# Linformer attention and a maxout layer on one core: the first batch in halves of its queries and heads, loads in that order, and a new order of its layers

## Chip, cores, metric

One core of a Trainium2 chip. The metric is device time in microseconds (us) of the whole program, the median over runs. The profile's "span" is one execution from its first to its last instruction, about 2 us less than the time. Engines: TensorE (PE; PEld is its weight load), VectorE (DVE), ScalarE (ACT), GpSimd (POOL, which here issues loads), SyncE (SP, which issues stores). The array is TensorE's matmul array. It is called cold, or at half clock, where a matmul takes twice its time elsewhere, and warm, or at full clock, otherwise; the granted clock is what the profile records of this, 1.00 being full.

## The reference

```python
# q, k, v: (8 batches, 8 heads, 1024, 64); E, F: (64, 1024); w1, w2: (512, 1024); w_out: (1024, 512)
k_proj = einsum('ks,bhsd->bhkd', E, k);  v_proj = einsum('ks,bhsd->bhkd', F, v)
attn = softmax(q @ k_proj^T / 8)                    # 64 keys per head
x    = (attn @ v_proj) as (8192 tokens, 512)
out  = maximum(x @ w1, x @ w2) @ w_out              # float32
```

Both kernels use max(h1, h2) = relu(h1 - h2) + h2. So there is one *up* layer with wd = w1 - w2, and the *down* layer adds relu(...) @ w_out and x @ m, where m = w2 @ w_out is computed once, in batch 0.

## The kernel before

A batch is a list of *slots*, each a few dense matmuls; between them stand the attention steps of the next batch. The program gives each engine its own instructions in a fixed order, its queue. Only batch 0 has nothing to hide its own attention behind. That opening is what the change concerns.

```python
for h0 in (0, H // 2):                          # batch 0: k, v of four heads, then of the other four
    load(tiles[0], "k", k, 0, h0, h0 + H // 2)
    load(tiles[0], "v", v, 0, h0, h0 + H // 2)
for h0 in range(0, H, 2):
    load(tiles[0], "q", q, 0, h0, h0 + 2)       # then q by head pairs
for f0 in range(0, DF, 256): ...                # then w2 and w1 in four pairs of pieces, then w_out
# steps: step_kv projects k and v of all heads; step_kpt and step_qt transpose; step_sc: scores, exp;
# step_da_half: sums and values, Ln, exp(-x), product into xt for one half of the tokens
step_kv(t); step_kpt(t); step_qt(t, 0); step_sc(t, 0)
for p in range(NP2):                            # four head pairs
    if p + 1 < NP2:
        step_qt(t, p + 1); step_sc(t, p + 1)
    step_da_half(t, p, 0)()
    step_w2t(256 * p)                           # transpose a piece of w2 (copy on ACT)
    step_wd(256 * p)                            # w1 - w2 (DVE)
# ... slots of batch 0: 8 up (half 0), m = w2 @ w_out, down (half 0), 8 up (half 1), down (half 1);
#     the second halves of step_da_half between the first up slots
```

The softmax here doesn't subtract the row's maximum and nothing guards it: scores larger than these inputs give would overflow.

## Time and profile before

| | before |
|---|---|
| time, median of 4 runs | 380.91 us (380.29 to 381.39) |
| profiled span | 378.3 us |
| TensorE busy | 353.2 us, 93% |
| first up layer can complete | 40.55 us |
| first up layers of batch 1 start | 92.62 us |
| projection in batch 1 starts | 99.53 us |

From 40.55 us on TensorE does not wait. This is the view of the waits of TensorE between 40 and 95 us, whole; the columns are engine and tile that waited, for whom, us in total, how often, the longest:

```profile
PE mm_ps L280 <- DVE xt_sb L263: 0.8, 1, 0.8
```

That wait is the one that ends at 40.55 us; after it there is none. The reading of the opening is in the prediction.

### The profile page before, as it was taken

The page shows a single profiled execution, that of the slowest core. Times are in us where ns is not written, and L with a number is a line of the kernel's source. Part 1 is how long each engine was busy: PE and PEld are TensorE (multiplying, and loading weights), DVE is VectorE, ACT ScalarE, POOL GpSimd, SP SyncE. Part 2 cuts the span into 40 slices and gives each one's busy share as a digit, 9 for nine tenths or more (in the row PEclk, how much of TensorE's full clock was granted, in tenths as well). Part 3 has the DMA queues.
Part 4 walks back from the last instruction along what each step waited for, and adds up shares of the span by engine and source line. Part 5 has one row for each costly group of instructions (what it writes and reads, how often), then busy time and mean ns, then how long its engine had stood idle before and what let it go on. Part 6 is the DMA issues. An engine that isn't in the chain of part 4 may idle for free.

```text
span 378.3 us, 4743 instructions
## 1 busy us (share of the span) xinstructions
PE 353.2 (93%) x1968; PEld 149.3 (39%) x1968; DVE 149.8 (40%) x211; ACT 152.0 (40%) x202; POOL 31.8 (8%) x44
## 2 busy tenths in 40 slices
PE   2375999999999999999999999999999999999996
PEld 2142344444434344344433444334433443344442
DVE  1034741453608172444425260716245351625040
ACT  1046634455154603653255505551355325460201
POOL 7362010000200002000200011000000000000000
PEclk9998999999999999999999999999999999999999
DMA  8999999969699267965599259936110332020202
GB/s 156 203 197 205 207 207 213 239 116 197 124 198 232 68 166 110 248 117 147 85 224 184 85 139 182 234 88 169 55 57 28 122 74 105 7 81 30 104 27 93
DMA packets 64469, 52.21 MB, mean 138 GB/s; under 512 B 26432, under 2 KB 56128, under 8 KB 64448
## 3 DMA queue, kind: packets, MB, share of 16 engines
q0 software_dynamic: 30304, 28.31, 47.6%
q1 hardware_dynamic: 34144, 23.60, 20.2%
q8 instruction: 15, 0.25, 0.2%
q14 instruction: 6, 0.05, 0.0%
HBM read 57.15 MB, written 16.78 MB: 195 GB/s over the span
## 4 chain that ended last, share of the span: by engine, by line
PE 90%; DMA 3%; ACT 3%; DVE 2%; issue 1%; POOL 1%; ACTq 0%; POOLq 0%
PE mm_ps L301 45%; PE mm_ps L280 30%; PE mm_ps L147 4%; PE att_ps L225 4%; DMA v_sb<-in_v_dram 3%; PE att_ps L206 3%; PE mm_ps L345 2%; ACT ex_sb L214 1%; PE mm_ps L180 1%; DVE qt_sb L187 1%; ACT rech_sb L260 1%; ACT ldh_sb L259 1%; PE att_ps L251 1%; PE mm_ps L161 0%; DVE wd_sb L323 0%
## 5 line engine op out<-in xcount | busy, mean ns | idle before, releaser
L301 PE MATMUL mm_ps<-wo_sb,gt_sb 128*128 128x512 f16 x512 | 123.8, 380 | 0.0
L280 PE MATMUL mm_ps<-xt_sb,wd_sb 128*128 128x512 f16 x512 | 116.6, 380 | 0.8 <-DVE xt_sb L263 0.8
L286 DVE TENSOR_SCALAR gt_sb<-mm_ps 128x512 f16<-128x512 f32 x128 | 87.1, 689 | 40.5 <-PE mm_ps L280 40.5
L237 DVE TENSOR_TENSOR xt_sb<-att_ps,rec_sb 128x1024 f16<-128x1024 f32 x28 | 34.3, 1224 | 113.7 <-ACT rec_sb L234 113.7
L280 PEld LDWEIGHTS <-wd_sb 128*128 128x128 f16 x512 | 47.9, 98 | 61.8 <-issue 7.7
L301 PEld LDWEIGHTS <-gt_sb 128*128 128x128 f16 x512 | 47.8, 98 | 61.9 <-issue 8.5
L301 PE MATMUL mm_ps<-m_sb,xt_sb 128*128 128x512 f16 x256 | 65.9, 380 | 0.0
L308 ACT COPY o_sb<-mm_ps 128x512 f32<-128x512 f32 x64 | 37.3, 582 | 69.9 <-PE mm_ps L301 60.5
L233 ACT ACTIVATE ld_sb<-att_ps 128x1024 f32<-128x1024 f32 x28 | 28.7, 1024 | 55.3 <-PE att_ps L225 55.3
L214 ACT ACTIVATE ex_sb<-att_ps 128x1024 f16<-128x1024 f32 x32 | 32.9, 1027 | 8.6 <-PE att_ps L206 8.6
L301 PEld LDWEIGHTS <-xt_sb 128*128 128x128 f16 x256 | 23.3, 98 | 31.4 <-issue 5.8
L154 ACT CAST kp_sb<-mm_ps 64x512 f16<-64x512 f32 x8 | 4.6, 580 | 63.1 <-PE mm_ps L147 63.1
L234 ACT ACTIVATE rec_sb<-ld_sb 128x1024 f32<-128x1024 f32 x28 | 29.6, 1056 | 0.9
L147 PE MATMUL mm_ps<-k_sb,eft 128*64 128x512 f16 x64 | 17.2, 413 | 6.8 <-DMA k_sb<-in_k_dram 6.8
L90 POOL DMA_DIRECT2D k_sb<-in_k_dram x9 | 7.8, 865 | 155.2 <-PE mm_ps L147 153.3
L206 PE MATMUL att_ps<-qt_sb,kpt_sb 64*64 64x512 f16 x128 | 13.6, 414 | 6.5 <-DVE qt_sb L187 6.5
L147 PE MATMUL mm_ps<-v_sb,eft 128*64 128x512 f16 x64 | 17.0, 413 | 1.9 <-DMA v_sb<-in_v_dram 1.9
L155 DVE CAST vp_sb<-mm_ps 64x512 f16<-64x512 f32 x8 | 5.6, 694 | 26.1 <-ACT kp_sb L154 26.1
L147 PEld LDWEIGHTS <-eft 128*64 128x64 f16 x128 | 7.3, 116 | 17.9 <-issue 13.6
L90 POOL DMA_DIRECT2D q_sb<-in_q_dram x11 | 9.1, 836 | 30.3 <-PE mm_ps L180 29.9
L225 PE MATMUL att_ps<-ex_sb,ones 64*64 64x512 f16 x112 | 11.5, 400 | 0.0
L206 PEld LDWEIGHTS <-kpt_sb 64*64 64x64 f16 x128 | 3.9, 104 | 19.0 <-issue 13.6
(41 smaller groups left out, 126.7 us busy)
## 6 DMA issues: line engine op xcount, KB each, us to landing
out_dram<-o_sb SPq DMA_DIRECT2D x64, 256.0 KB, 2.0
k_sb<-in_k_dram POOLq DMA_DIRECT2D x7, 1024.0 KB, 11.8
v_sb<-in_v_dram POOLq DMA_DIRECT2D x7, 1024.0 KB, 18.2
q_sb<-in_q_dram POOLq DMA_DIRECT2D x7, 1024.0 KB, 21.6
w_sb<-in_moe_w_dram POOLq DMA_DIRECT2D x8, 256.0 KB, 10.4
k_sb<-in_k_dram POOLq DMA_DIRECT2D x2, 512.0 KB, 8.6
v_sb<-in_v_dram POOLq DMA_DIRECT2D x2, 512.0 KB, 10.5
q_sb<-in_q_dram POOLq DMA_DIRECT2D x4, 256.0 KB, 13.5
```

Of the source, the lines that this page charges most:

```text
L90: nc.gpsimd.dma_start(out=t[n][:, h0:h1, :, :], in_=src[b, h0:h1].rearrange("h (p c) d -> p h c d", c=NC),)
L147: nc.tensor.matmul(out=kv_ps[i * KP : (i + 1) * KP, :], lhsT=eft[:, i, c, :], rhs=t[n][:, :, c, :], start=(c == 0), stop=(c == NC - 1),)
L206: nc.tensor.matmul(out=sc_ps[pos : pos + KP, e, :], lhsT=t["kpt"][o * D : (o + 1) * D, 2 * p + e, :], rhs=t["qt"][o * D : (o + 1) * D, 2 * ...
L214: nc.scalar.activation(out=ex, in_=sc_ps, func=ACTF.Exp, scale=scale)
L225: nc.tensor.matmul(out=dst[e * D : (e + 1) * D, o, :], lhsT=ones16[rows, :] if w is None else w[rows, 2 * p + e, :], rhs=ex[rows, e, :], s ...
L233: nc.scalar.activation(out=ld, in_=dn_ps, func=ACTF.Ln)
L234: nc.scalar.activation(out=rec, in_=ld, func=ACTF.Exp, scale=-1.0)
L237: nc.vector.tensor_tensor(out=t["xt"][:, p, :, :], in0=at_ps, in1=rec, op=ALU.mult)
L280: nc.tensor.matmul(out=h_ps, lhsT=wd_sb[:, r, fb * 128 : (fb + 1) * 128], rhs=xt[:, r, j, :], start=(r == 0), stop=(r == NDC - 1),)
L286: nc.vector.tensor_scalar_max(gt[:, fb, :], h_ps, 0.0)
L301: nc.tensor.matmul(out=op_ps, lhsT=lhsT, rhs=rhs, start=(n == 0), stop=(n == NFB + NDC - 1),)
L308: nc.scalar.copy(out=o_sb, in_=op_ps)
```

## The change

Its intent: start the first batch's attention when half of its heads have landed, compute it only for half of the query blocks before the up layers start, and put the rest between up layers. Both up layers then come first, m next, the down layers last. The next batch's attention moves later (slot 23 on, it was 7 on), since its time in the up layers is taken by the second half of this batch.

```diff
+    load(k, heads 0-3); load(v, heads 0-3)
+    load(q, heads 0-3, first half of the query blocks)
+    load(k, heads 4-7); load(v, heads 4-7)
+    load(q, heads 4-7, first half of the query blocks)
     for f0 in range(0, DF, 256):
+        if f0 == 512:
+            load(tiles[0], "q", q, 0, 0, H, NC // 2, NC)      # the other half of q
... (the calls of load are shortened; the cut parts give the steps ranges of heads and blocks)
+    for g in range(2):                                        # two groups of four heads
+        p0 = 2 * g
+        step_kv(t, 4 * g, 4 * g + 4)
+        step_kpt(t, p0, p0 + 2)
+        step_qt(t, 4 * g, 4, 0, NI // 2)
+        step_sc(t, p0, 0)
+        step_sc(t, p0 + 1, 0)
+        if g == 1:
+            step_wd(0)
+        fin = step_da_half(t, p0, 0)
+        fin()
+        if g == 1:
+            step_wd(256)
+        fin = step_da_half(t, p0 + 1, 0)
+        fin()
+    first = {                                                 # what follows which slot
+        0: [(step_wd, 512)],
+        1: [(step_qt, t, 0, 4, NI // 2, NI), (step_sc, t, 0, 1)],
+        2: [(step_qt, t, 4, 4, NI // 2, NI), (step_sc, t, 1, 1), (step_wd, 768)],
+        3: [(step_da_half, t, 0, 1)],  4: [(step_sc, t, 2, 1)],  5: [(step_da_half, t, 1, 1)],
+        6: [(step_sc, t, 3, 1)],  7: [(step_da_half, t, 2, 1)],  9: [(step_da_half, t, 3, 1)],
+    }
... step_w2t copies on DVE instead of ACT; in batch 0:
+            ups = [*up_slots(t, 0), *up_slots(t, 1)]
+            seq = ups[:NFB] + [four step_w2t]
+            seq += ups[NFB:] + [four step_m]
+            seq += [*down_slots(b, t, 0), *down_slots(b, t, 1)]
```

More of the change, by code (lines that the diff above doesn't have):

```diff
@@ L87, in alloc_kvq, with load @@
         return t
-    def load(t, n, src, b, h0, h1):
+    def load(t, n, src, b, h0, h1, c0=0, c1=NC):
         nc.gpsimd.dma_start(
-            out=t[n][:, h0:h1, :, :],
-            in_=src[b, h0:h1].rearrange("h (p c) d -> p h c d", c=NC),
+            out=t[n][:, h0:h1, c0:c1, :],
+            in_=src[b, h0:h1].rearrange("h (p c) d -> p h c d", c=NC)[:, :, c0:c1, :],
         )
     tiles = {0: alloc_kvq()}
-    for h0 in (0, H // 2):
-        load(tiles[0], "k", k, 0, h0, h0 + H // 2)
-        load(tiles[0], "v", v, 0, h0, h0 + H // 2)
-        if h0 == 0:
-            ident = const.tile([128, 128], FP32)
-            make_identity(nc, ident)
-    for h0 in range(0, H, 2):
-        load(tiles[0], "q", q, 0, h0, h0 + 2)
+    load(tiles[0], "k", k, 0, 0, H // 2)
+    load(tiles[0], "v", v, 0, 0, H // 2)
+    ident = const.tile([128, 128], FP32)
+    make_identity(nc, ident)
+    load(tiles[0], "q", q, 0, 0, H // 2, 0, NC // 2)
+    load(tiles[0], "k", k, 0, H // 2, H)
+    load(tiles[0], "v", v, 0, H // 2, H)
+    load(tiles[0], "q", q, 0, H // 2, H, 0, NC // 2)
     w1_sb = const.tile([128, NDC, DF], FP16)
@@ L140, in new_attn, with step_kv, step_kpt @@
         t["xt"] = xpool.tile([128, NP2, 2, HALF], FP16, tag="xt", name="xt_sb")
+        t["qt"] = qtp.tile([128, H, HALF], FP16, tag="qt", name="qt_sb")
         t["ex"] = {}
-    def step_kv(t):
+    def step_kv(t, h0=0, h1=H):
         kv_ps = mm_bank()
+        n = (h1 - h0) * D
         for c in range(NC):
-            for i, n in enumerate(("k", "v")):
+            for i, w in enumerate(("k", "v")):
                 nc.tensor.matmul(
-                    out=kv_ps[i * KP : (i + 1) * KP, :],
+                    out=kv_ps[i * KP : (i + 1) * KP, 0:n],
                     lhsT=eft[:, i, c, :],
-                    rhs=t[n][:, :, c, :],
+                    rhs=t[w][:, h0:h1, c, :],
                     start=(c == 0), stop=(c == NC - 1),
                 )
-        fl = lambda ap: ap.rearrange("p h d -> p (h d)")
-        nc.scalar.copy(out=fl(t["kp"]), in_=kv_ps[0:KP, :])
-        nc.vector.tensor_copy(out=fl(t["vp"][KP:128]), in_=kv_ps[KP:128, :])
-        nc.vector.tensor_copy(out=fl(t["vp"][0:KP]), in_=kv_ps[KP:128, :])
-    def step_kpt(t):
+        fl = lambda ap: ap[:, h0:h1, :].rearrange("p h d -> p (h d)")
+        nc.scalar.copy(out=fl(t["kp"]), in_=kv_ps[0:KP, 0:n])
+        nc.vector.tensor_copy(out=fl(t["vp"][KP:128]), in_=kv_ps[KP:128, 0:n])
+        nc.vector.tensor_copy(out=fl(t["vp"][0:KP]), in_=kv_ps[KP:128, 0:n])
+    def step_kpt(t, p0=0, p1=NP2):
         kpt_ps = mm_bank(FP16)
-        for p in range(NP2):
+        for p in range(p0, p1):
             nc.tensor.transpose(
-                out=kpt_ps[:, p * KP : (p + 1) * KP],
+                out=kpt_ps[:, (p - p0) * KP : (p - p0 + 1) * KP],
                 in_=t["kp"][:, 2 * p : 2 * p + 2, :],
@@ L165, in step_kpt @@
             )
-        src = kpt_ps[:, 0 : NP2 * KP].rearrange("q (p k) -> q p k", k=KP)
-        dst = t["kpt"].rearrange("q (p e) k -> q p e k", e=2)
+        src = kpt_ps[:, 0 : (p1 - p0) * KP].rearrange("q (p k) -> q p k", k=KP)
+        dst = t["kpt"][:, 2 * p0 : 2 * p1, :].rearrange("q (p e) k -> q p e k", e=2)
         for e in range(2):
@@ L174, in step_kpt, with step_qt @@
                 )
-    def step_qt(t, p):
+    def step_qt(t, h0, nh=2, i0=0, i1=NI):
         qt_ps = mm_bank(FP16)
-        for e in range(2):
-            for i in range(NI):
+        ni = i1 - i0
+        for h in range(nh):
+            for i in range(ni):
                 nc.tensor.transpose(
-                    out=qt_ps[:, (e * NI + i) * 128 : (e * NI + i + 1) * 128],
-                    in_=t["q"][:, 2 * p + e, 2 * i : 2 * i + 2, :],
+                    out=qt_ps[:, (h * ni + i) * 128 : (h * ni + i + 1) * 128],
+                    in_=t["q"][:, h0 + h, 2 * (i0 + i) : 2 * (i0 + i) + 2, :],
                     identity=ident16,
                 )
-        if "qt" not in t:
-            t["qt"] = qtp.tile([128, H, HALF], FP16, tag="qt", name="qt_sb")
         nc.vector.tensor_copy(
-            out=t["qt"][:, 2 * p : 2 * p + 2, :].rearrange("q e n -> q (e n)"), in_=qt_ps
+            out=t["qt"][:, h0 : h0 + nh, i0 * 128 : i1 * 128],
+            in_=qt_ps[:, 0 : nh * ni * 128].rearrange("q (h n) -> q h n", h=nh),
         )
     def step_qt_dma(t):
-        t["qt"] = qtp.tile([128, H, HALF], FP16, tag="qt", name="qt_sb")
         nc.sync.dma_start_transpose(
@@ L197, in step_qt_dma, with step_sc @@
         )
-    def step_sc(t, p):
+    def step_sc(t, p, j=None):
         sc_ps = att_banks()
+        n = slice(0, HALF) if j is None else slice(j * HALF // 2, (j + 1) * HALF // 2)
+        w = n.stop - n.start
         for o in range(2):
@@ L206, in step_sc @@
                 nc.tensor.matmul(
-                    out=sc_ps[pos : pos + KP, e, :],
+                    out=sc_ps[pos : pos + KP, e, 0:w],
                     lhsT=t["kpt"][o * D : (o + 1) * D, 2 * p + e, :],
-                    rhs=t["qt"][o * D : (o + 1) * D, 2 * p + e, :],
+                    rhs=t["qt"][o * D : (o + 1) * D, 2 * p + e, n],
                     start=True, stop=True,
@@ L213, in step_sc @@
         t["ex"][p] = ex
-        nc.scalar.activation(out=ex, in_=sc_ps, func=ACTF.Exp, scale=scale)
+        nc.scalar.activation(
+            out=ex[:, :, 0:w], in_=sc_ps[:, :, 0:w], func=ACTF.Exp, scale=scale
+        )
     def step_da(t, p):
@@ L241, in step_da, with step_da_half @@
         return finish
-    def step_da_half(t, p, o):
-        ex = t["ex"][p]
+    def step_da_half(t, p, j):
+        ex = t["ex"].pop(p)
+        W = HALF // 2
         da_ps = att_banks()
         for i in range(2):
-            for e in range(2):
-                r = o ^ e
-                rows = slice(r * KP, (r + 1) * KP)
-                nc.tensor.matmul(
-                    out=da_ps[e * D : (e + 1) * D, i, :],
-                    lhsT=t["vp"][rows, 2 * p + e, :] if i else ones16[rows, :],
-                    rhs=ex[rows, e, :],
-                    start=True, stop=True,
-                )
-        ld = soft.tile([128, HALF], FP32, tag="ldh", name="ldh_sb")
-        rec = soft.tile([128, HALF], FP32, tag="rech", name="rech_sb")
-        nc.scalar.activation(out=ld, in_=da_ps[:, 0, :], func=ACTF.Ln)
+            for r in range(2):
+                for e in range(2):
+                    o = r ^ e
+                    rows = slice(r * KP, (r + 1) * KP)
+                    nc.tensor.matmul(
+                        out=da_ps[e * D : (e + 1) * D, o, i * W : (i + 1) * W],
+                        lhsT=t["vp"][rows, 2 * p + e, :] if i else ones16[rows, :],
+                        rhs=ex[rows, e, 0:W],
+                        start=True, stop=True,
+                    )
+        ld = soft.tile([128, 2, W], FP32, tag="ldh", name="ldh_sb")
+        rec = soft.tile([128, 2, W], FP32, tag="rech", name="rech_sb")
+        nc.scalar.activation(out=ld, in_=da_ps[:, :, 0:W], func=ACTF.Ln)
         nc.scalar.activation(out=rec, in_=ld, func=ACTF.Exp, scale=-1.0)
@@ L263, in finish @@
             nc.vector.tensor_tensor(
-                out=t["xt"][:, p, o, :], in0=da_ps[:, 1, :], in1=rec, op=ALU.mult
-            )
-        return finish
-    def moe_slots(b, t):
-        xt = t["xt"]
-        for j in range(2):
-            gt = gpool.tile([128, NFB, HALF], FP16, tag="gt", name="gt_sb")
-            for fb in range(NFB):
-                def up(fb=fb, j=j, gt=gt):
-                    h_ps = mm_bank()
-                    for r in range(NDC):
-                        nc.tensor.matmul(
-                            out=h_ps,
-                            lhsT=wd_sb[:, r, fb * 128 : (fb + 1) * 128],
-                            rhs=xt[:, r, j, :],
-                            start=(r == 0), stop=(r == NDC - 1),
-                        )
-                    nc.vector.tensor_scalar_max(gt[:, fb, :], h_ps, 0.0)
-                yield up
-            for i in range(NI):
-                cell = {}
-                toks = slice(i * 128, (i + 1) * 128)
-                for part in range(3):
-                    def down(i=i, j=j, gt=gt, cell=cell, toks=toks, part=part):
-                        if part == 0:
-                            cell["ps"] = mm_bank()
-                        op_ps = cell["ps"]
-                        for n in range(4 * part, 4 * part + 4):
-                            if n < NFB:
-                                lhsT, rhs = gt[:, n, toks], wo_sb[:, n, :]
-                            else:
-                                lhsT, rhs = xt[:, n - NFB, j, toks], m_sb[:, n - NFB, :]
-                            nc.tensor.matmul(
-                                out=op_ps, lhsT=lhsT, rhs=rhs,
-                                start=(n == 0), stop=(n == NFB + NDC - 1),
-                            )
-                        if part < 2:
-                            return
-                        o_sb = opool.tile([128, DM], FP32, tag="o", name="o_sb")
-                        nc.scalar.copy(out=o_sb, in_=op_ps)
-                        nc.sync.dma_start(
-                            out=out.rearrange("(n p c) m -> n p c m", p=128, c=NC)[
-                                b, :, 2 * i + j, :
-                            ],
-                            in_=o_sb,
-                        )
-                    yield down
@@ L318 @@
+                out=t["xt"][:, p, :, j * W : (j + 1) * W],
+                in0=da_ps[:, :, W : 2 * W], in1=rec, op=ALU.mult,
+            )
+        return finish
     wd_sb = const.tile([128, NDC, DF], FP16)
@@ L320, with up_slots, up, down_slots @@
     w2t_sb = const.tile([128, NFB, DM], FP16)
+    def up_slots(t, j):
+        W = HALF // 2
+        t["gt", j] = gt = gpool.tile([128, NFB, HALF], FP16, tag="gt", name="gt_sb")
+        for fb in range(NFB):
+            def up(fb=fb):
+                h_ps = mm_bank()
+                for r in range(NDC):
+                    nc.tensor.matmul(
+                        out=h_ps,
+                        lhsT=wd_sb[:, r, fb * 128 : (fb + 1) * 128],
+                        rhs=t["xt"][:, r, :, j * W : (j + 1) * W],
+                        start=(r == 0), stop=(r == NDC - 1),
+                    )
+                nc.vector.tensor_scalar_max(gt[:, fb, :], h_ps, 0.0)
+            yield up
+    def down_slots(b, t, j):
+        for n2 in range(NI):
+            o, i = n2 % 2, 2 * j + n2 // 2
+            cell = {}
+            g0 = (o * 2 + n2 // 2) * 128
+            for part in range(3):
+                def down(o=o, i=i, g0=g0, cell=cell, part=part):
+                    gt = t["gt", j]
+                    if part == 0:
+                        cell["ps"] = mm_bank()
+                    op_ps = cell["ps"]
+                    for n in range(4 * part, 4 * part + 4):
+                        if n < NFB:
+                            lhsT, rhs = gt[:, n, g0 : g0 + 128], wo_sb[:, n, :]
+                        else:
+                            lhsT = t["xt"][:, n - NFB, o, i * 128 : (i + 1) * 128]
+                            rhs = m_sb[:, n - NFB, :]
+                        nc.tensor.matmul(
+                            out=op_ps, lhsT=lhsT, rhs=rhs,
+                            start=(n == 0), stop=(n == NFB + NDC - 1),
+                        )
+                    if part < 2:
+                        return
+                    o_sb = opool.tile([128, DM], FP32, tag="o", name="o_sb")
+                    nc.scalar.copy(out=o_sb, in_=op_ps)
+                    nc.sync.dma_start(
+                        out=out.rearrange("(n p c) m -> n p c m", p=128, c=NC)[
+                            b, :, 2 * i + o, :
+                        ],
+                        in_=o_sb,
+                    )
+                yield down
     def step_wd(f0):
@@ L337, in step_w2t @@
         fb = f0 // 128
-        nc.scalar.copy(
+        nc.vector.tensor_copy(
             out=w2t_sb[:, fb : fb + 2, :].rearrange("q f m -> q (f m)"), in_=ps_t
@@ L353 @@
     new_attn(t)
-    step_kv(t)
-    step_kpt(t)
-    step_qt(t, 0)
-    step_sc(t, 0)
-    for p in range(NP2):
-        if p + 1 < NP2:
-            step_qt(t, p + 1)
-            step_sc(t, p + 1)
-        step_da_half(t, p, 0)()
-        step_w2t(256 * p)
-        step_wd(256 * p)
+    for g in range(2):
[17 more added lines that the diff above has]
+        2: [(step_qt, t, 4, 4, NI // 2, NI), (step_sc, t, 1, 1), (step_wd, 768)],
+        3: [(step_da_half, t, 0, 1)],
+        4: [(step_sc, t, 2, 1)],
+        5: [(step_da_half, t, 1, 1)],
+        6: [(step_sc, t, 3, 1)],
+        7: [(step_da_half, t, 2, 1)],
+        9: [(step_da_half, t, 3, 1)],
+    }
     core = {
@@ L371 @@
     }
-    by_pe = {11: (step_qt, 0), 16: (step_qt, 1), 22: (step_qt, 2), 28: (step_qt, 3)}
+    late = {
+        23: (step_kv,), 24: (step_kpt,), 25: (step_qt, 0), 27: (step_qt, 2), 28: (step_sc, 0),
+        31: (step_da, 0), 32: (step_qt, 4), 33: (step_sc, 1), 36: (step_da, 1),
+        37: (step_qt, 6), 38: (step_sc, 2), 41: (step_da, 2), 43: (step_sc, 3), 45: (step_da, 3),
+    }
     by_dma = {1: (step_qt_dma,)}
@@ L382 @@
             new_attn(nxt)
-            steps = {**core, **(by_dma if b else by_pe)}
-        pending = None
-        for n, slot in enumerate(moe_slots(b, tiles[b])):
-            if b == 0 and n == NFB:
-                for r in range(NDC):
-                    step_m(r)
-            slot()
-            if pending is not None:
-                pending()
-                pending = None
-            if b == 0 and n % 2 == 0 and n < 2 * NP2:
-                pending = step_da_half(tiles[0], n // 2, 1)
-            if n in steps:
-                s = steps[n]
-                pending = s[0](nxt, *s[1:])
+            steps = {n: [(s[0], nxt, *s[1:])] for n, s in (
+                {**core, **by_dma} if b else late).items()}
+        t = tiles[b]
+        if b == 0:
+            ups = [*up_slots(t, 0), *up_slots(t, 1)]
+            seq = ups[:NFB] + [lambda f0=f0: step_w2t(f0) for f0 in range(0, DF, 256)]
+            seq += ups[NFB:] + [lambda r=r: step_m(r) for r in range(NDC)]
+            seq += [*down_slots(b, t, 0), *down_slots(b, t, 1)]
+            steps.update(first)
+        else:
+            seq = [s for j in range(2) for f in (up_slots(t, j), down_slots(b, t, j)) for s in f]
+        pending = []
+        for n, slot in enumerate(seq):
+            slot()
+            for f in pending:
+                f()
+            pending = []
+            for s in steps.get(n, ()):
+                r = s[0](*s[1:])
+                if r is not None:
+                    pending.append(r)
+        for f in pending:
+            f()
         del tiles[b]
```

## The prediction

> **What bounds the kernel now.** I read the page's busy slices first, then the chain of waits in order of time, then the timeline of the first 60 us, then busy time by stretch.
>
> ```profile
> PE   2375999999999999999999999999999999999996
> DMA  8999999969699267965599259936110332020202
> ```
> Each digit is a fortieth of the span (9.46 us), in tenths. TensorE (PE) is full from the fifth slice on; only the first four have room. The stretches agree (start and end, length, then PE busy):
>
> ```profile
> 0.00:13.78 13.78, 2.26 (x16) 1.94 (x17) 1.03 (x3) 1.87 (x2) 8.11 (x16) 1.00 0.99 170
> 13.78:40.55 26.77, 16.84 (x120) 9.06 (x120) 9.09 (x16) 13.37 (x19) 10.56 (x13) 0.94 1.33 202
> 40.55:92.62 52.07, 52.07 (x306) 21.81 (x306) 22.85 (x33) 24.61 (x35) 2.63 (x3) 1.00 1.10 197
> ```
> The third is the rest of batch 0, without a gap in PE. A change of opening can only win in the first 40.55 us. The chain there, with pieces left out:
>
> ```profile
> 4.17 11.98 DMA v_sb<-in_v_dram
> 16.29 3.60 PE mm_ps L147 x15
> 19.91 0.59 ACT kp_sb L154
> ...
> 22.47 0.70 DVE qt_sb L187
> 23.22 0.64 PE att_ps L206 x4
> ...
> 26.30 1.02 ACT ex_sb L214
> 27.32 0.50 ACT ldh_sb L259
> 27.84 0.64 ACT rech_sb L260
> ...
> 39.80 0.70 DVE xt_sb L263
> 40.55 0.38 PE mm_ps L280
> ```
> So: wait to 16.29 for all of k and v (all heads in one projection), then a chain of small steps through ACT, DVE and PE, until the last head pair's xt lets the first up layer finish at 40.55. When loads land shows in whom the issuing engine waited for (bracket: idle before, and what ended it):
>
> ```profile
> 8.58 0.74 POOL L110 DMA_DIRECT2D w_sb<-in_moe_w_dram  x1 [0.84 <-DMA k_sb<-in_k_dram]
> 11.41 0.74 POOL L110 DMA_DIRECT2D w_sb<-in_moe_w_dram  x1 [2.08 <-DMA v_sb<-in_v_dram]
> 17.71 0.74 POOL L110 DMA_DIRECT2D w_sb<-in_moe_w_dram  x1 [0.54 <-DMA q_sb<-in_q_dram]
> 19.05 0.74 POOL L110 DMA_DIRECT2D w_sb<-in_moe_w_dram  x1 [0.60 <-DMA q_sb<-in_q_dram]
> ```
> The first half of k's heads is there at 8.58, of v's at 11.41; each further 512 KB takes about 2.5 us, each 256 KB about 1.3.
>
> **What the Trainium skill says.** "TensorE: Matmul & The Clock Gate", Part 1: the array runs at half clock until a free-running window of about 3.4 us was busy. The trace agrees: k/v pairs of 512 columns start every 0.43 us at 16.3-18.9 and every 0.21 us at 49.5; PE is slow again near 35.3 after idling, and fast from about 38.7. "ScalarE: Activation LUTs", What ACT_TABLE_LOAD costs: an activation with immediate operands takes 186 ns plus 0.833 ns per element, so halving a tile does not halve it. Here 1024 elements took 1.024 us and 512 took 0.595: agreed. "DMA: Bandwidth & Descriptors", Specifications: lines of 512 B or more go at line rate. The quarter loads of q get 512 B lines; the weight pieces have such lines already, and their 256 KB take the same 1.3 us as q's 1 KB lines. So reordering costs no bandwidth. "TensorEngine Tiling (Array Packing)", Key Properties: a change of tiling mode drains the array. Eight down matmuls after such a step take 1.83 us in the chain, 1.73 otherwise; more small steps cost about 0.1 us each.
>
> **The change, part by part.**
>
> *Loads.* k, v of four heads, then a quarter of q, then the same for the other heads, then two weight pairs, the other half of q, two more pairs. Estimated landings from the rates above: k 8.6, v 11.4, q 12.7, k 15.1, v 17.6, q 18.9, weight pairs complete at 21.6 and 24.3, q's rest 26.9, third pair 29.5, fourth 32.2. Bytes are unchanged, so w_out and the next batch land as before.
>
> *Opening.* First group, at the half clock: v at 11.4; 8 pairs of 256 columns, 8 x 0.213 + 0.3 = 2.0, to 13.4; kp cast 0.37 (0.58 less 256 elements) and two transposes, 14.2; meanwhile q's eight transposes (1.04) to 15.2; qt copy 0.69, 15.95; scores, exp from 16.45; two exps of 0.6 to 17.55; sums and values; Ln and exp(-x) of 0.6 + 0.64 per pair, on ACT one after the other to 20.2. PE takes the second projection meanwhile: from 18.2, when the first group's values are out (v landed at 17.6, so the chain and not the DMA sets this), to 20.3. Then the same ladder: kp 20.7, transposes 22.15, qt 22.9, exps 23.4 to 24.5, ACT's Ln/exp for two pairs to 27.15, and on DVE a product (0.6), one wd piece (0.6), the last product, to 27.9. **First up layer complete to go at 28.0 instead of 40.55: 12.5 us earlier.**
>
> *What is given back.* Left for later, in PE time at full clock: w2's transposes 4 x 0.45 = 1.8; half of q's transposes 2 x 0.45 = 0.9; second halves of the scores 4 x 0.23 = 0.9. The later sums and values get cheaper (four 64x64 tiles at once, as in the later batches, where 8 matmuls of 512 take 0.56): 4 x 0.34 instead of 4 x 0.55, -0.8. Net 2.8 us. If PE never waited, the gain would be 12.5 - 2.8 = 9.7.
>
> *Waits that I expect.* DVE runs in order: gt0, wd piece 3 (needs the load of 29.5), gt1, copy of q's second half, and only then the scores of slot 1, which stand ahead of up layer 2 in PE's queue. With gt1 at 30.1-30.75 and the copy to 31.4, PE goes on at 31.45; at full clock it has been through slot 1 and its transposes at 29.65: 1.8 us. Before up layer 8 (second half) DVE still has two products and w2t copies, 0.69 each and moved from ACT: the last product ends about 43.15, PE is there at about 42.1: 1.1 us. At the end of batch 0, the last sums start after slot 45 of 48, and Ln 1.02, exp 1.06, product 1.22 plus 0.5 of latencies (3.8) face two slots of 0.865, the last part of the sums' own matmuls and three up matmuls of 0.216 (together 2.7): about 0.9 us (there were five slots before, no wait). Small-step drains: some eight more at 0.08, 0.6. Sum 4.4: gain **9.7 - 4.4 = 5.3 us** if PE is at full clock when the up layers start. If it is cold (it idles most of 25 to 28), the following 3.4 to 6.8 us run at half speed; part of it lies beside the DVE wait, so it costs up to 1.7 more. Against that, a warm second group would save 0.6, and part of the drains falls in waits. I take 5.3 less 0.6 for the clock plus 0.7 for those: 5.4 us.
>
> *Rest.* Batches 1 to 7 keep their slots, matmul counts and sizes; xt is read as two runs of 256 columns, at the same count of columns. I count zero.
>
> Time: 381.15 - 5.4 = **375.7 us**, 1.4% less.
>
> **The rivals.** (a) *DVE becomes the bound in batch 0's up layers.* Sixteen evictions and four copies, four products, two q copies, two wd pieces: 28 x 0.61 = 17.1 us of DVE, beside 13.8 of up matmuls and about 5.3 of small PE steps, 19.1. So DVE is near the bound but under it; if each order mismatch costs something, gain 2 to 3 us, 378.5. For it: the trace shows 0.61 from start to start for evictions back to back. Against it: seven us of w2 @ w_out and the down layers follow, without DVE work of that size. (b) *The loads set the start anyway.* Weight pairs three and four need bytes that land at 29.5 and 32.2 in any order; if loads slipped 2 us through finer pieces, the up layers stall on DVE and the gain falls to 3.5. For it: DMA is at 9 tenths there. Against it: same bytes and line rates, and the third pair is needed by up layer 4 only. (c) *The opening is gained whole*: warm clock, no wait at the second half, gain 8 to 9, about 372.5. For it: the PE work alone allows 9.7; against it: the three waits above come from the order of instructions, not from luck. (d) *Nothing gained because later waits move up*: the next batch's projections run at slot 23 rather than 7, so loads for batch 3, whose buffers they free, are issued at about 59 instead of 51.7; they are due after 130, so this is hidden.
>
> **Range and chances.** The opening is uncertain by about 1 us each way, the clock by 1.5, the waits by 1.5: gains of 3 to 8 us should hold eight times in ten, 373.2 to 378.1. Faster by over 2% needs more than 7.6 us: 0.16. Slower by over 2% would need a wait in every batch: 0.02.
>
> **What would show it.** Right: the first up matmul with the last xt product near 28 (27 to 29.5); a PE wait of 1 to 2 us for the qt copy before the second scores, one of about 1 us for the last xt product of the second half, and one under 1 us at the first up layer of batch 1, which starts near 87 instead of 92.6; from there on the same 41.25 us per batch. Wrong: the up layers starting after 31 (chain or loads mis-sized), PE waits in the up layers summing to over 5 us (rival a), or a batch period other than 41.25 us.

## The result

| | before | changed |
|---|---|---|
| time, median of 4 runs | 380.91 us | 376.78 us (375.64 to 376.80) |
| ratio to before | | 0.9885 (95%: 0.9861 to 0.9909) |
| profiled span | 378.3 us | 375.0 us |
| first up layer can complete | 40.55 us | 27.66 us |
| projection in batch 1 starts | 99.53 us | 96.31 us |

A ratio here is the mean time of one kernel's runs over that of the other's of the same rounds, so not quite the ratio of the medians quoted. The gain is 1.2%, some 4 us, while the opening is 12.9 us shorter. Where did 9 us go?

The page of the changed kernel, busy tenths; TensorE's is to be held against 2375999 in the kernel before:

```profile
PE   2668999999999999999999999999999999999996
```

TensorE's waits from 27 to 92 us, whole, in the same columns as above:

```profile
PE mm_ps L296 <- DVE xt_sb L274: 2.1, 3, 0.9
PE att_ps L213 <- DVE qt_sb L192: 1.2, 1, 1.2
PE mm_ps L296 <- DVE xt_sb L246: 0.8, 1, 0.8
```

Where there was one wait, there are three kinds. Of the 2.1 us in the first line only 0.89 lie after 27.66 us, so 2.87 us of waits follow the opening, where the kernel before has none. The chain of waits in order of time shows them in their places (start, length, what). Tiles: wd is w1 - w2, gt the output of an up layer, qt the transposed q, xt the output of the attention, w2t the transposed w2:

```profile
30.06 0.69 DVE wd_sb L340
30.75 0.60 DVE gt_sb L302
31.35 0.61 DVE qt_sb L192
...
32.01 0.43 PE att_ps L213 x2
32.43 1.82 PE mm_ps L296 x4
34.25 0.85 PE mm_ps L187 x8
...
35.47 1.20 PE mm_ps L296 x4
...
37.01 0.97 PE mm_ps L296 x4
...
43.38 0.69 DVE xt_sb L274
44.07 1.20 DVE w2t_sb L355 x2
45.27 0.61 DVE xt_sb L274
...
45.91 6.42 PE mm_ps L296 x29
...
88.61 1.24 DVE xt_sb L246
...
89.89 6.42 PE mm_ps L296 x29
```

- At 30.06 VectorE at last gets the third weight pair (it came out of the DMA queue then), evicts an up layer, copies q, and only then can the second scores start, at 32.01. TensorE stood 1.20 us.
- Four up matmuls take 1.82 us at 32.43, but 0.97 at 37.01: the array is at half clock until about 35.8 us (of the four at 35.47, which take 1.20, one is still slow).
- At 45.91 the first up layer of the second half gets the last product, which had stood in VectorE's queue behind two copies of w2's transposes.
- At 89.89 the first up layer of batch 1 waits for the last product of that batch's attention, 0.78 us.

The clock has to be read from durations here. The busy times by stretch give, in the third number from the end, the granted clock; this stretch reads as full, though the lines above show half:

```profile
27.66:35.60 7.94, 6.74 (x34) 3.28 (x34) 3.73 (x6) 0.68 (x2) 2.73 (x4) 1.00 1.34 202
```

### The profile page after: what moved, and what is told of

It is laid out like the page before. It is cut to its first block, busy times and chain, and to the rows that moved or that the text cites. A ratio compares the mean times of both kernels' runs of the same rounds, so it can differ in the third digit from the quotient of the medians. Undisturbed runs are those within 1.5% of the kernel's fastest.

```text
span 375.0 us, 4882 instructions
## 1 busy us (share of the span) xinstructions
PE 354.8 (95%) x2032; PEld 151.6 (40%) x2032; DVE 153.3 (41%) x219; ACT 149.5 (40%) x205; POOL 31.4 (8%) x43
## 4 chain that ended last, share of the span: by engine, by line
PE 89%; DMA 7%; DVE 2%; ACT 1%; POOL 1%; issue 0%; ACTq 0%; DVEq 0%; POOLq 0%
PE mm_ps L322 45%; PE mm_ps L296 30%; PE att_ps L234 4%; PE mm_ps L152 3%; DMA v_sb<-in_v_dram 3%; DMA w_sb<-in_moe_w_dram 3%; PE att_ps L213 3%; PE mm_ps L362 2%; PE mm_ps L187 1%; PE mm_ps L166 0%; DVE xt_sb L274 0%; DVE xt_sb L246 0%; DVE w2t_sb L355 0%; POOL k_sb L90 0%; ACT rec_sb L243 0%
## 5 line engine op out<-in xcount | busy, mean ns | idle before, releaser
L296 PE MATMUL mm_ps<-xt_sb,wd_sb 128*128 128x512 f16 x512 | 119.7, 386 | 2.9 <-DVE xt_sb L274 2.1
L221 ACT ACTIVATE ex_sb<-att_ps 128x1024 f16<-128x1024 f32 (+1 forms) x36 | 33.3, 931 | 15.8 <-PE att_ps L213 15.7
L159 ACT CAST kp_sb<-mm_ps 64x512 f16<-64x512 f32 (+1 forms) x9 | 4.8, 532 | 57.0 <-PE mm_ps L152 57.0
L152 PE MATMUL mm_ps<-v_sb,eft 128*64 128x512 f16 (+1 forms) x72 | 17.2, 390 | 2.5 <-DMA v_sb<-in_v_dram 2.5
L152 PE MATMUL mm_ps<-k_sb,eft 128*64 128x512 f16 (+1 forms) x72 | 17.4, 390 | 1.5 <-DMA k_sb<-in_k_dram 1.5
L213 PE MATMUL att_ps<-qt_sb,kpt_sb 64*64 64x512 f16 (+1 forms) x144 | 14.2, 396 | 3.2 <-DVE qt_sb L192 3.2
L160 DVE CAST vp_sb<-mm_ps 64x512 f16<-64x512 f32 (+1 forms) x9 | 5.7, 635 | 26.7 <-ACT kp_sb L159 26.7
L152 PEld LDWEIGHTS <-eft 128*64 128x64 f16 x144 | 8.7, 122 | 12.2 <-issue 6.1
L234 PE MATMUL att_ps<-ex_sb,vp_sb 64*64 64x512 f16 x112 | 10.8, 376 | 0.0
```

The costliest lines, as they stand in the source:

```text
L152: nc.tensor.matmul(out=kv_ps[i * KP : (i + 1) * KP, 0:n], lhsT=eft[:, i, c, :], rhs=t[w][:, h0:h1, c, :], start=(c == 0), stop=(c == NC - 1),)
L213: nc.tensor.matmul(out=sc_ps[pos : pos + KP, e, 0:w], lhsT=t["kpt"][o * D : (o + 1) * D, 2 * p + e, :], rhs=t["qt"][o * D : (o + 1) * D, 2 ...
L221: nc.scalar.activation(out=ex[:, :, 0:w], in_=sc_ps[:, :, 0:w], func=ACTF.Exp, scale=scale)
L234: nc.tensor.matmul(out=dst[e * D : (e + 1) * D, o, :], lhsT=ones16[rows, :] if w is None else w[rows, 2 * p + e, :], rhs=ex[rows, e, :], s ...
L296: nc.tensor.matmul(out=h_ps, lhsT=wd_sb[:, r, fb * 128 : (fb + 1) * 128], rhs=t["xt"][:, r, :, j * W : (j + 1) * W], start=(r == 0), stop= ...
```

## The experiments

Each is an edit of the changed kernel unless said otherwise, and all gave the reference's result. "Wait" is TensorE's, from the trace of one run.

| run | time, median (range), us | ratio to before |
|---|---|---|
| changed kernel again | 375.46 (374.79 to 376.92) | 0.9881 |
| next batch's attention earlier | 376.38 (374.40 to 376.81) | 0.9890 |
| second scores later | 373.92 (373.70 to 375.57) | 0.9840 |
| old order of layers | 376.27 (374.80 to 377.53) | 0.9891 |
| TensorE kept warm | 375.98 (374.42 to 377.51) | 0.9889 |
| w2's transposes fill the gap | 374.75 (374.41 to 375.71) | 0.9860 |
| w2's copies back on ACT | 378.73 (377.86 to 379.08) | 0.9960 |
| old loads | 379.63 (379.06 to 381.01) | 0.9994 |
| third weight pair first | 376.18 (375.35 to 377.00) | 0.9875 |
| three edits together | 374.06 (373.29 to 374.71) | 0.9821 |
| three edits, m ahead of the second up layers | 372.73 (372.47 to 374.03) | 0.9795 |
| kernel before, new loads alone | 385.71 (385.15 to 388.14) | 1.0139 |

The intervals are 0.0013 to 0.0029 on either side. One us is 0.0026.

### The changed kernel again

> The changed kernel unaltered, to see how far it moves from one run to the next. Theory (the opening is 12.5 us shorter and 9 us of that are given back by moved work, waits and a cold clock): span 374 to 375.5 us, ratio to the kernel before 0.987 to 0.991, and batch 1 starting near 88 us. Rival (the 1.1% was luck of the chip or of the clock's phase): a ratio outside 0.985 to 0.993.

The ratio repeated, 0.9881. But all nine runs of the changed kernel fall into two kinds: 374.79, 375.43, 375.46, 375.64, and 376.58, 376.77, 376.79, 376.80, 376.92. The first trace (above) is of a 376.77 run, this one of a 375.43 run. TensorE's instructions in this one, in time order:

```profile
29.78 1.06 PE L187 MATMUL mm_ps<-ident,q_sb 128*128 128x128 f16 x8
32.42 0.30 PE L213 MATMUL att_ps<-qt_sb,kpt_sb 64*64 64x256 f16 x4 [1.58 <-DVE qt_sb L192]
32.65 1.04 PE L296 MATMUL mm_ps<-xt_sb,wd_sb 128*128 128x512 f16 x4
...
44.59 0.59 PE L296 MATMUL mm_ps<-xt_sb,wd_sb 128*128 128x512 f16 x2 [0.89 <-DVE xt_sb L274]
```

Here the four up matmuls at 32.65 are already fast (1.04 us from the first's start to the last's end; 1.89 in the slow trace). Though its weight pair landed 0.4 us later, the second half's up layer was released 1.32 us earlier, at 44.59 instead of 45.91. From there to the first up layer of batch 1 both took 43.98 us. So the kinds differ in when the half clock ends, shown by these two traces; that all nine runs divide for this reason is likely, not shown.

### The next batch's attention earlier

```diff
-        31: (step_da, 0), ... 36: (step_da, 1), ... 41: (step_da, 2), 43: (step_sc, 3), 45: (step_da, 3),
+        29: (step_da, 0), ... 33: (step_da, 1), ... 37: (step_da, 2), 39: (step_sc, 3), 41: (step_da, 3),
```

> The next batch's attention steps in batch 0 are moved up so that its last sums start after slot 41 instead of 45. Theory (the last Ln, exp and product of batch 1's attention outlast the slots left and hold TensorE up at batch 1's first up layer): that wait of 0.78 us disappears, 0.7 to 0.9 us less than the changed kernel, no new wait over 0.3 us. Rival (the wait is only a symptom, and the closer steps wait for the attention banks): the wait appears in the down layers instead, and the time stays within 0.3 us.

In the trace the wait at batch 1 is gone and no new one stands among the down layers. The projection of batch 1 starts at 93.93 us, against 94.99 in the trace just above; 0.11 of that was there before the edit's place. So the wait was real and worth about 0.95 us. The median does not show it: its runs are 374.40, 374.59, and four from 376.15 to 376.81, more of the slow kind than the control had. By time alone, this run is inconclusive.

### The second scores later

```diff
-        1: [(step_qt, t, 0, 4, NI // 2, NI), (step_sc, t, 0, 1)],
-        2: [(step_qt, t, 4, 4, NI // 2, NI), (step_sc, t, 1, 1), (step_wd, 768)],
+        1: [(step_qt, t, 0, 4, NI // 2, NI)],
+        2: [(step_sc, t, 0, 1), (step_qt, t, 4, 4, NI // 2, NI), (step_sc, t, 1, 1), (step_wd, 768)],
```

> The first second-half scores are issued one up layer later, so that an up layer stands between the transposes of q and the scores that need their copy. Theory (TensorE waits 1.2 us there because VectorE is held by the weight piece that lands at 30 us, and the queue is in order): 1.0 to 1.6 us less than the changed kernel, and the up layers of the second half start that much sooner. Rival (VectorE or the loads bound the whole stretch): the wait moves to the next eviction or to the first up layer of the second half, which still completes near 46 us, and the time stays within 0.3 us.

1.5 us less than the control's median. The first up layer of the second half is released at 43.05 us (44.59 in the control's trace), and keeps its wait of 0.9 us. The scores, which stood in TensorE's queue ahead of an up layer that could run, were the whole of the wait. VectorE is not the bound of the stretch. The release in the chain, to be held against 45.91 above:

```profile
43.05 6.42 PE mm_ps L296 x29
```

### The old order of layers

```diff
-            seq += ups[NFB:] + [lambda r=r: step_m(r) for r in range(NDC)]
-            seq += [*down_slots(b, t, 0), *down_slots(b, t, 1)]
+            seq += [lambda r=r: step_m(r) for r in range(NDC)] + [*down_slots(b, t, 0)]
+            seq += ups[NFB:] + [*down_slots(b, t, 1)]
```

> Only the order of batch 0 goes back: up layers of the first half, w2 @ w_out, down layers of the first half, up layers of the second, down layers of the second; the new opening stays. Theory (the second half's first up layer waits 0.9 us for the last product, which is late because its chain starts only at slot 9): that wait goes, 0.8 to 1.0 us less than the changed kernel; the wait at batch 1 stays at 0.6 to 0.9. Rival (the order with both up layers first is needed to keep TensorE fed while w_out and the next batch land): a wait of over 1 us for w_out or for the next k and v, and a time 1 us or more above the changed kernel.

Neither time came. The wait for the last product is gone, as the theory had it, but m now comes right after w2's transposes and waits for their last copy:

```profile
44.59 1.68 PE L362 MATMUL mm_ps<-wo_sb,w2t_sb 128*128 128x512 f16 x7 [0.59 <-DVE w2t_sb L355]
```

No load starves the old order, and the time is that of the new one (0.9891 against 0.9881). On top of the new opening, the order of the layers is worth nothing that these runs resolve.

### TensorE kept warm

```diff
+    dummy(4) before the second group's scores, dummy(2) after them, dummy(8) after its sums and values
+    # dummy(n): n matmuls, 256 columns, results unread
```

> The changed kernel with 14 matmuls of 256 columns whose results nobody reads, put into TensorE's idle stretches between 21 and 27 us. Theory (the unaltered kernel has two kinds of runs, near 375.0 and 376.7 us, because the array's half clock ends sometimes near 32 and sometimes near 35.5 us, after the up layers have begun at 27.7): the array is at full clock when or soon after the up layers start, in every run; no run above 375.6 us although there is more work, median 374.0 to 375.2. Rival (the two kinds come from the loads, say the third weight pair landing earlier or later): still two kinds 1.5 to 2 us apart, both up to 0.5 us slower for the added work.

My theory fell in its main point. The array was warm as wished; the first up layers ran at full clock, the q transposes at 28.47 took 0.61 us instead of 1.06. And then:

```profile
32.19 0.33 PE L213 MATMUL att_ps<-qt_sb,kpt_sb 64*64 64x256 f16 x4 [3.11 <-DVE qt_sb L192]
32.45 1.89 PE L296 MATMUL mm_ps<-xt_sb,wd_sb 128*128 128x512 f16 x4
```
```profile
32.20:35.50 3.30, 3.30 (x21) 1.63 (x22) 0.96 (x2) 0.60 (x1) 0.01 (x1) 0.52 1.25 208
```

TensorE arrived sooner at the same wait, stood 3.11 us instead of 1.2, and went cold in it: the granted clock of the next 3.3 us is 0.52. The copy of q comes when VectorE gets its weight pair, whatever TensorE does. In this trace, being fast ahead of a fixed wait bought a longer wait and the half clock behind it. The runs spread from 374.42 to 377.51, wider than the two kinds that the rival wanted.

### w2's transposes fill the gap

```diff
         fin = step_da_half(t, p0 + 1, 0)
+        if g == 1: step_w2t(0)
         fin()
+        if g == 1: step_w2t(256); step_wd(256)      # step_wd(256) stood ahead of step_da_half
```

> Half of w2's transposes move from after the first up layers into TensorE's idle stretch before them (25 to 27 us), and the second weight piece behind the last product. Theory (that stretch waits for ACT and VectorE, so TensorE work fits in for nothing, and keeps the clock up): 0.9 us of transposes and two copies leave the middle; 0.6 to 1.2 us less than the changed kernel's median, fewer runs of the slow-clock kind. Rival (their copies sit in VectorE's queue between the last products and hold the first up layer up): the first up layer is complete 0.6 us or more later than at 27.7 and the time is the same within 0.3 us.

0.9860, about 0.8 us less than the changed kernel's 0.988: as expected, and all four runs are at or below 375.71, though the intervals of the two ratios overlap. The first up layer was complete to go at 28.19 us, 0.5 later than in the first trace, which was the rival's sign; but the second group's projection had started 0.65 later too (18.46 against 17.81), so this trace does not lay it on the copies. In the trace the second scores still come at 32.32 us, after a wait of 2.4 us, so part of what it won is spent there.

### w2's copies back on ACT

```diff
-        nc.vector.tensor_copy(
+        nc.scalar.copy(
             out=w2t_sb[:, fb : fb + 2, :]..., in_=ps_t
```

> Only the four copies of w2's transposes go back from VectorE to ACT. Theory (at this point the last product waits for ACT's Ln and exp, ACT's queue is in order, and a copy takes 0.99 us there): the last product of the second half ends 0.8 to 1.6 us later, the first up layer of the second half with it, and the time rises by 0.8 to 1.6 us. Rival (VectorE bounds the up layers): four copies of 0.6 us less on VectorE bring the second half's first up layer 0.6 to 1.8 us forward, and the time falls by as much.

The direction is the theory's, the size double: about 3 us slower. The trace says why. The last product comes late, because its Ln waits on ACT behind a copy, and TensorE stands 1.99 us. Then the granted clock is 0.52 and 0.70 in the two stretches up to 50 us:

```profile
42.60 1.02 ACT w2t_sb L355
43.62 0.51 ACT ldh_sb L270
...
45.55 8.10 PE mm_ps L296 x29
```

```profile
45.50:47.50 2.00, 1.95 (x5) 0.69 (x5) 0.69 (x2) 1.09 (x2) 0.00 (x0) 0.52 1.24 205
47.50:50.00 2.50, 2.50 (x9) 0.97 (x8) 1.31 (x2) 0.00 (x0) 0.00 (x0) 0.70 1.25 208
```

The wait is 1.1 us longer than the control's, and the clock it costs adds 1.7 us: the stretch of 29 matmuls that follows takes 8.10 us in the chain, against 6.42 in the changed kernel. So moving these copies to VectorE was a needed part of the change.

### Old loads

```diff
-    q in halves of its query blocks between k, v of the two groups; its rest between the weight pairs
+    k, v, k, v by four heads; q by head pairs; the weights
```

> The order and size of the loads go back (k, v, k, v by heads, then q by head pairs, then the weights), the steps stay as changed. Theory (the opening chain starts when four heads' k, v and q are there): the first scores wait for the second q load, near 19 us instead of 12.7; the first up layer is complete at 31 to 33 instead of 27.7 us, of which the wait for the third weight pair near 30 us hides a part: 2.5 to 4.5 us slower than the changed kernel, so most of the gain is lost. Rival (the smaller steps are what matters and the order of loads does not, since the weights land at the same time): the same within 0.5 us.

All of the gain is lost. The first four heads of k and v were ready as in the changed kernel (their transposes done by 13.6 us), but q was not:

```profile
17.37 0.61 PE L185 MATMUL mm_ps<-ident,q_sb 128*128 128x128 f16 x4 [3.78 <-DMA q_sb<-in_q_dram]
18.63 0.60 PE L185 MATMUL mm_ps<-ident,q_sb 128*128 128x128 f16 x4 [0.66 <-DMA q_sb<-in_q_dram]
```

The first up layer could complete at 32.07 us instead of 27.66. The delay of 4.4 us arrived in the time nearly whole.

### Third weight pair first

```diff
-        if f0 == 512:
+        if f0 == 768:
             load(tiles[0], "q", q, 0, 0, H, NC // 2, NC)
```

> The third weight pair is loaded ahead of the second half of q instead of behind it; nothing else differs. Theory (after the first up layers TensorE stands still because VectorE's queue waits for that pair, which lands near 30 us): the pair lands near 27.3 us and the second half of q near 29.7; the wait for the copy of q goes from 1.2-1.6 us to under 0.9, the second scores start at 30.9 to 31.5 instead of 32.0 to 32.4, and the time falls by 0.7 to 1.4 us. Rival (the half clock is what holds this stretch): the second scores start at 32 or later as before and the time is the same within 0.4 us.

A miss. The pair came early: VectorE made its wd piece at 28.80 without waiting. But q's rest, now behind it, came at 30.5 and not 29.7:

```profile
30.52 1.03 PE L187 MATMUL mm_ps<-ident,q_sb 128*128 128x128 f16 x8 [0.66 <-DMA q_sb<-in_q_dram]
32.34 0.43 PE L213 MATMUL att_ps<-qt_sb,kpt_sb 64*64 64x256 f16 x4 [0.78 <-DVE qt_sb L192]
```

The second scores start at 32.34 us as before, and the time is the same (0.9875). Both the pair and q's rest are needed before these scores, and whichever is sent last lands past 30 us. The wait can be covered with other work, as the later scores did; neither of these two orders of loads removes it. Not run: both loads ahead of the second pair, or the copy of q ahead of the weight piece in VectorE's queue. The rival's time came true, its reason in small part: the loads hold the transposes back to 30.52, and their half clock adds some 0.4 us (1.03 instead of 0.61).

### Three edits together, with and without m ahead

```diff
 (second scores later) + (w2's transposes fill the gap) + (next batch's attention earlier)
 and in the second of the two:
-            seq += ups[NFB:] + [lambda r=r: step_m(r) for r in range(NDC)]
+            seq += [lambda r=r: step_m(r) for r in range(NDC)] + ups[NFB:]
```

> Three of the edits together: the second scores one up layer later, half of w2's transposes in the opening, the next batch's attention steps up to four slots earlier. Theory (three separate waits, at 30, at 43 and at 88 us, each given back once): 1.5 + 0.6 + 0.9 = 3.0 us less than the changed kernel's median of 375.5 to 376.8, so 372.3 to 373.8, and 0.979 to 0.983 of the kernel before. Rival (one wait takes the place of another): 374 or more.

> The same three edits, and w2 @ w_out ahead of the up layers of the second half, so that its 7 us cover the last product. Theory: the wait of 0.8 us before the second half's first up layer goes, and if the last two copies of w2's transposes come late they cost up to 0.7 us ahead of w2 @ w_out: 0.1 to 0.8 us less than the three edits alone, 371.8 to 373.5. Rival (that product was late because VectorE is full): w2 @ w_out waits just as long for its copies, and the time is the same within 0.2 us.

The three gave 0.9821, within the expected ratio, at its slow edge; in us the 374.06 lies just above what I had written, and just inside the rival's "374 or more". The sum of the single gains is not reached, and the trace shows the rival's reason, one wait in place of another: with transposes in the opening TensorE is warm and early again, waits 2.5 us for the copy of q, and two later up layers run cold (1.72 and 1.71 us for four matmuls). With m ahead the ratio is 0.9795 and the median 372.73 us, the fastest, 1.3 us below the other where 0.1 to 0.8 was expected (the intervals of the ratios overlap). TensorE's waits from the trace's first 100 us show both sides of it:

```profile
PE att_ps L213 <- DVE qt_sb L192: 4.3, 3, 2.3
...
PE mm_ps L362 <- DVE w2t_sb L355: 1.2, 2, 0.6
```

The wait for the last product is replaced by two of 0.6 us for w2's copies. In waits alone that is no gain, as the rival said. In this trace the array stayed at full clock after the 2.3 us wait, which it had not in the trace without m ahead. From the first up layer to batch 1's projection the two traces take 66.23 and 68.02 us; of the 1.79 between, 1.58 are the cold matmuls and 0.24 the shorter wait for q's copy, so these two leave nothing for the order. How much of the 1.3 us between the medians is the order and how much the clock's luck is open.

### The kernel before, with the new loads alone

```diff
+    the changed kernel's order and sizes of loads
     (all steps as in the kernel before)
```

> The kernel before with the new loads only; its steps still project all heads at once and take q whole. Theory (the new loads pay only with steps that can use half of the heads and half of q): the projection starts 1.3 us later, near 17.6 us, the first transposes of q wait for the rest of q near 27 us instead of about 21, and the first up layer moves from 40.5 to 45 us or more: 3.5 to 6.5 us slower than the kernel before. Rival (the order of the loads carries the gain alone, since undoing it cost all of it): at or below the kernel before.

4.8 us slower than before. TensorE waited 4.3 us for q's rest in the middle of the first transposes, and the first up layer could complete at 47.15:

```profile
27.99 0.82 PE L181 MATMUL mm_ps<-ident,q_sb 128*128 128x128 f16 x6 [4.32 <-DMA q_sb<-in_q_dram]
```

Steps without loads gave 0.9994, loads without steps 1.0139, both 0.988: each half of the change is worth nothing or less without the other.

## Why the prediction was right, and where it was not

The time was forecast as 375.7 us, and it was 376.78; the gain 5.4 us, and it was 4.1 by medians (4.4 by the ratio). Its steps, against the first trace and that of the control:

| step | predicted | first trace (376.77 us) | control (375.43 us) |
|---|---|---|---|
| first up layer complete to go | 28.0 | 27.66 | 27.69 |
| third weight pair | 29.5 | 30.06 | 30.47 |
| second scores | 31.45 | 32.01 | 32.42 |
| last product of the second half | 43.15 | 45.87 | 44.55 |
| wait at batch 1's first up layer | about 0.9 | 0.78 | 0.78 |

**The opening** was right within 0.4 us: the ladder of small steps, with the chain and not the loads setting it. The second group's projection started at 17.81 without a wait, and GpSimd, which waited for the same v, went on at 18.01 (17.6 estimated); the two were closer than I had them.

**What was given back** can be summed from the same traces. From the first up layer to batch 1's projection the kernel before takes 58.98 us, the first trace 68.65, the control 67.30:

| us more than before | predicted | first trace | control |
|---|---|---|---|
| up to the second scores, over the 1.69 that this work takes warm | 1.8 | 2.66 | 3.04 |
| half clock after the second scores (all of the prediction's 0.6 is put here) | 0.6 | 1.73 | 0 |
| wait for the last product | 1.1 | 0.89 | 0.89 |
| wait at batch 1 | 0.9 | 0.78 | 0.78 |
| the rest: work moved, drains | 2.8 + 0.6 - 0.7 | 3.61 | 3.61 |
| sum | 7.1 | 9.67 | 8.32 |

(1.69 is from the trace kept warm, 27.39 to 29.08; the rest is what is left of the sum.) So the parts are those forecast, and the waits are where they were put. "Later scores" showed that the first wait is one of order, and "earlier attention" the same for batch 1. For that last wait the prediction's own terms, 3.8 against 2.7, make 1.1 and not its 0.9; the chain to the product took 3.45 us and TensorE's work beside it 2.67. From batch 1's projection to the end nothing changed: 278.8 us before, 278.7 in both traces.

**Three terms were too small.** The time up to the second scores: the third weight pair came 0.56 and 0.97 us later than forecast and the first up layer 0.3 earlier, so more had to be waited. The credit of 0.7 us, for a warm second group and drains inside waits, which does not show: the second group's transposes of q took 1.04 us, cold, and the last row is nearer to 3.4 than to 2.7. And, in the slow kind, the clock. I took 0.6 us for it, allowing up to 1.7. In the first trace the cold array costs after 32.01: first scores 0.13, up layer 0.85 (1.82 less 0.97), transposes 0.40 (0.85 less 0.45), scores 0.13, up layer 0.23; 1.7 us on the path. It was at half clock from before 27.66 to about 35.8, 8 us, where the prediction's estimate was 3.4 to 6.8. In the control it was warm by the second scores and cost nothing after them; there the first two terms (1.24 and 0.91 too small) outweigh that. Five of the nine runs are of the slow kind. The warm experiment adds what I had not seen: the clock and the wait are not two terms to be summed. Warm before the wait means a longer wait, and it can mean cold after it.

**The rivals.** (a), VectorE as the bound, is refuted by "later scores", which gained 1.5 us with the same VectorE work; "copies on ACT", which took work off VectorE, lost 3 us. (b), the loads: half right. Their landing at 30 us does hold the second scores, and the one other order tried does not help, but other work covers it. (c), the whole opening kept, did not happen for the reasons given. (d), the next batch's loads, never showed as a wait in any trace.

Still open: what a run's clock phase depends on, and whether the changed kernel can be kept in its fast kind.

## What to carry to other kernels

Splitting the first batch paid here only with loads and steps split alike; check each alone. A saved opening is a budget that the following slots can spend again: for every engine, list its queue in order after the change, and put an independent block of work between a producer on another engine and the consumer that waits for it. Where a wait's end is set by a load, making the waiting engine faster ahead of it gained nothing here; give it other work instead.

## What the Trainium skill lacked or had wrong

- "TensorE: Matmul & The Clock Gate", Why this matters for your kernels, advises "No PE-idle gaps >~3µs between matmul bursts". Here a wait of 1.99 us was followed by a granted clock of 0.52 and 0.70 in the two stretches of the next 4.5 us, while one of 2.3 us in another run was not. Shorter gaps were not safe here, and their cost (1.7 us) exceeded the excess of the wait (1.1 us). Transposes stood shortly ahead of the 1.99 us; whether they count as work for the clock is not shown.
- The same page, Part 4, says that full clock "doesn't engage" for transpose mode. Eight 128x128 transposes (nc.tensor.transpose) took 0.85 us in the chain before the array was warm and 0.45 us after, so they do run faster on a warm array; whether they help to warm it is not shown.
- The same page, Part 1, warns in general that the clock events in a trace can be unreliable; no page read names what was met here, a granted clock that reads as full while the array is at half: 1.00 for 27.66 to 35.60 us, with four matmuls of 512 columns at 1.82 us in place of 0.97. In such a stretch durations have to be read instead.
- The same page, Part 1, puts the warm-up penalty under 1% of a typical kernel's span and advises against fitting a count of cold matmuls. The size holds here: 1.7 us on the path in the first trace, about 0.5%. But the change itself is 1.2%, so in a comparison of this size the term cannot be left out.
